# Five more quads of exponentials on VectorE, another filler for TensorE, and new ScalarE costs in the planner of a transformer block

## The chip, the cores and the metric

One core of a Trainium2 chip runs the kernel, in one launch. The metric is the time of one execution in microseconds on the device; less is better.

## What is computed

A transformer block with conditioning: layer norm and modulation, attention with 32 heads of 16, then layer norm, modulation and a gated feed-forward network (FFN), each with a gated residual. Cut to what matters (S = 2048, D = 512, H = 32, F = 1792, all bfloat16):

```python
mod = silu(c) @ w_mod                       # six rows of 512: sa, ca, ga, sb, cb, gb
h = layernorm(x) * (1 + ca) + sa
q, k, v = split(h @ wqkv)                   # 32 heads of 16
p = softmax(q @ k.T * 16 ** -0.5)           # 32 heads x 2048 x 2048
x = x + ga * ((p @ v) @ wo)
h = layernorm(x) * (1 + cb) + sb
x = x + gb * ((gelu(h @ w_gate) * (h @ w_up)) @ w_down)
```

The softmax has 32 x 2048 x 2048 exponentials, 134 million, or 2048 banks of 128 partitions by 512 columns.

## The kernel before, in words

The program is written by a planner that runs at build time. Every operation goes through `rec`, which finds its dependences and places it in a model of the engines' times (`model`, `cost`); `probe` asks when an operation could begin. `stream` is the planner's loop: at each turn it puts the next piece of TensorE work in order, and the order it finds is fixed in the program. No time is decided on the chip; engines wait for each other by semaphores.

Queries are cut into sets (`SETS`): seven of 256 queries and two of 128, where sets 0 and 1, and the last two, go together as 512 and 256 queries for the first four units. A unit is a set and one of eight groups of four heads (`qd`). A round of a unit is one bank of 512 columns for each of its four heads (`j`): scores are matmuls of kT against qT (even groups) or qo (odd groups) into `ps_sc`, six banks used as two sets of three (`CH`). ScalarE's exponential (`ACT.Exp`, through `act`, line 338) takes a set of two or three banks into a ring of 15 slots, `E`. Up to `nsplit` (the first two units, over all keys) every second set has two banks, because one bank holds the second unit's sum.

A round can instead be a quad: VectorE makes the bits of the bfloat16 exponential from each of its four banks (`ts` with `SHIFT_C`, line 350) into a `kq` buffer, one bank with each turn of the loop, so that ScalarE gets two banks and VectorE the third. The approximation is averaged over four shifts: three more buffers (`sq`) are made from `kq` by adding a number to the bits (`shift_task`, 128x2048), and each goes with a scaled copy of the values, `vs`. So a quad has 4 exps and 3 shifts on VectorE, and four times the PV matmuls of a plain round. Before, rounds were candidates for a quad (`cand`) only over the last four tiles of keys (`T0 = 12`), not in the first two units, and not until `modB` is there; `vs` holds those four tiles alone and is scaled when the last v is there (end of `side_v`).

PV matmuls (17 rows: 16 of v and a row of ones) add into `ps_pv`, or into the sixth score bank for the second unit (`pv_mms`, `acc_of`). When a unit ends, `unit_end` copies its sum to `osb` (line 359), and its sums of exponentials are inverted, spread through DRAM and multiplied in.

Side work is a list of generators with due positions (`plan`, `advance`): normalisation and q, k, v projections in the first stretch (`side_first`, `side_dc`, `side_q_all`), then for each set the output projection (`side_wo`), LN2 statistics and normalisation on VectorE (`ln2_steps`), its transposes (`side_t2`) and the FFN (`side_ffn`). It uses one bank, `ps_mi`, for its sums; `self.open` says that a sum is open there. The rate is a credit that grows with the position. VectorE's small work waits in `tasks`, taken by urgency (`step`).

`short` counts the columns that TensorE streamed in a window before now. Where they are under `FILL`, the planner adds filler: matmuls of the identity with one tile of xs, into a free score bank, or into `ps_mi` if no sum is open there.

Of the kernel before, what the change touches and what calls it, by code (L numbers as in the profile page):

```python
# [35 lines left out]
QJ = 4  # L36
QS = 4
MERGED = (((0, 1), (2, 3), (4, 5), (6,), (7,)), ((0, 1), (2, 3), (4,), (5,), (6,), (7,)))
CH = 3
# [5 lines left out]
NK = 4  # L45
CREDIT = 3500
NS = 3
# [8 lines left out]
MARGIN = {"db": 1200, "dd": 1800, "de": 1500, "qo": 1500, "st": 1500, "sd": 1700, "wd": 1700, "wu": 1500, "wg": 1500}  # L56
BACK = 6
GAP = 120
END = (0, None)
# [30 lines left out]
class _Recorder:  # L90
# [207 lines left out]
    def cost(self, eng, out, ins, kind):  # L298
        n = 1
        for _, k in (out if kind != "bn" else ins[0]).ap[1:]:  # L300
            n *= int(k)
        aps = [out] + list(ins)
        ps = any(self.kind.get(a.tensor.name) == "ps" for a in aps)
        small = all(mybir.dt.size(a.dtype) == 2 for a in aps)
        if eng == "act":
            return n * 0.833 + (51 if ps else 92)
        if eng == "pool":
            return n * 3.0 + 100
        f = 1
# [121 lines left out]
class _Kernel(_Recorder):  # L431
# [12 lines left out]
    def alloc(self):  # L444
# [35 lines left out]
        self.kq = [dreg[:, 0:2048], dreg[:, 2048:4096], mreg[:, 12288:14336]]  # L480
        self.kq += [sb("kq%d" % i, [P, 2048], BF16)[:, :] for i in range(3, NK)]
        self.vs = sb("vs", [P, len(SHIFT), NKT - T0, H * VW], BF16)
        self.wo = sb("wo", [P, 7, D], BF16)
        self.E = sb("E", [P, NSL, 512], BF16)
        self.onorm = sb("onorm", [P, 8, 512], BF16)
        self.ga = sb("ga", [P, D], BF16)
# [19 lines left out]
        self.rm = sb("rm", [P, 2], FP32)  # L506
        self.ident = sb("ident", [P, P], BF16)
        self.ones = dreg[:, 10 * D:10 * D + P]
        self.half = dreg[:, 10 * D + P:10 * D + 2 * P]
# [7 lines left out]
    def prologue(self):  # L517
# [19 lines left out]
        half = self.half  # L537
        self.memset(dve, self.warm, 0.0)
        self.memset(dve, half[:, 0:2], 0.5)
        self.memset(dve, self.ones, 1.0)  # L540
# [69 lines left out]
    def prologue_v(self):  # L610
        self.ln_stat(5)
        self.proj_v(0, 0, self.mi[:, :])
        for t in range(4, 6):
            self.done(("st", t))
# [150 lines left out]
    def side_v(self, g, dc):  # L765
# [61 lines left out]
    def side_first(self):  # L827
# [260 lines left out]
    def side_ffn(self, gi, part=None):  # L1088
# [66 lines left out]
        def U(ci):  # L1155
# [4 lines left out]
            for b0 in range(0, m, kpb):  # L1160
# [7 lines left out]
                yield END  # L1168
        early = [part is not None]

        def near():
            if early[0] and ("osb", gi + 1, 5) in self.have:
                early[0] = False
                yield from self.near_end(gi + 1, 5, self.mi)
# [102 lines left out]
    def plan(self, ends, nsplit, begin):  # L1277
# [78 lines left out]
    def stream(self):  # L1356
# [40 lines left out]
        last = {u: g0 + 4 for u, r, g0 in rounds}  # L1397
        begin = [min(g0 for u, r, g0 in rounds if u[1] // 2 == x) for x in range(4)]
        self.work = self.plan(ends, nsplit, begin)
        self.slot = {}  # L1400
# [8 lines left out]
        for u, r, g0 in rounds:  # L1409
# [4 lines left out]
        wait = []  # L1414
        self.quad_free = list(range(NK))
        self.sq_free = list(range(NSQ))
        cand = [k for k, (u, r, g0) in enumerate(rounds)
                if u not in units[:2] and r * (512 // u[3]) >= T0]
        quad = None

        def take(n):
# [57 lines left out]
        def pv_do(x):  # L1479
# [10 lines left out]
            else:  # L1490
# [4 lines left out]
                if q["n"] == 0:  # L1495
                    wait.remove(q)
                    self.quad_free.append(q["k"])
            if left[u] == 0:
# [6 lines left out]
        while cg <= group[units[-1]]:  # L1505
            if parts and pos >= max(loaded, ends[FLOW - 1] + 8):
                x = next((x for x in parts if all(k in self.have for k in x[2])), None)
                if x is not None:
# [3 lines left out]
                    loaded = pos + (8 if x[1][1] != 1 else 2)  # L1512
            t = max(self.pe_now(), virt)
            for k in range(NSETS):
                if pos >= ends[k]:
                    self.done(("qk", k))
# [9 lines left out]
            if tq is not None and tq <= t + 30:  # L1526
                slack = self.free["act"] - 600 - t
                w = self.next_side()
# [6 lines left out]
                g = None  # L1535
                if len(mem) == CH and "modB" in self.have and self.free["dve"] < max(t + 700, self.free["act"] + 150):
                    while quad is None and cand and last[rounds[cand[0]][0]] < pos + AHEAD[rounds[cand[0]][0][3] == 512]:
                        cand.pop(0)
                    overdue = {x[1][1] for x in self.tasks if x[1] is not None and x[1][0] == "shift" and self.plain[x[1][1]] <= LATE}
                    if quad is not None:  # L1540
                        if not overdue - {quad["rnd"][0]}:
                            g = quad["rnd"][2]
                    elif (not overdue and cand and self.quad_free and (pos < ends[FLOW - 1] or self.credit < CREDIT or (self.next_side() is None and self.waiting[0] in ("onorm", "osb"))) and rounds[cand[0]][2] < pos + 96 and self.backlog() < BACK
                          and ("vs", rounds[cand[0]][0][1] // 2) in self.have
                          and all(k in self.have for k in self.keys(seq[rounds[cand[0]][2]]))):
                        rnd = rounds[cand.pop(0)]
                        quad = {"rnd": rnd, "j": [0, 1, 2, 3], "k": self.quad_free.pop(0), "ready": [], "n": NS + 1, "slots": {}}
                        left[rnd[0]] += NS
# [25 lines left out]
                if g is not None:  # L1574
# [5 lines left out]
                    at = self.probe(bits)  # L1580
                    while self.free["dve"] + GAP < at and self.step("dve", self.free["dve"] + 40):
                        pass
# [22 lines left out]
            if w is not None and pos >= w[1]:  # L1605
                ts = self.probe(w[4][1])
                n = w[4][0]
                side = (ts <= t + 30 and (self.credit >= n / 2 or "last" in self.have or (self.short(t) > 0 and self.credit > -2048))
                        and n / 2.4 <= gap + max(0, self.free["act"] - 600 - t - max(0, gap)))
            if ok[0] and (ok[1] or self.pe_mode == 2 or tq is None or not mem) and not (  # L1610
# [37 lines left out]
    def pv_mms(self, rnd, acc, src, i, first, last):  # L1648
# [11 lines left out]
    def shift_task(self, q, i):  # L1660

        def f():
            s = self.sq_free[0]
            self.ts("dve", self.sq[s].bitcast(U16), self.kq[q["k"]].bitcast(U16), float(SHIFT[i]), None, ALU.add)
            if self.probing is None:
                self.sq_free.pop(0)
                q["slots"][i + 1] = s
                q["ready"].append((i + 1, [self.sq[s][:, 512 * x:512 * x + 512] for x in range(4)]))
        self.task([f], ("shift", q["rnd"][0]), lambda: bool(self.sq_free))

# [11 lines left out]
    def unit_end(self, u, acc):  # L1682
# [3 lines left out]
        self.copy("dve", self.osb[:, lo:hi], acc[:, 0:W])  # L1686
        if sets[0] >= NSETS - 2 and len(sets) == 1 and qd >= (6 if sets[0] == NSETS - 2 else 5):
# [4 lines left out]
        if two and qd % 2 == 0:  # L1692
            return
        us = [u]
        if two:
            us, lo, b = [(sets, qd - 1, q0, W), u], lo - W, b - 1
# [267 lines left out]
```

## Time and profile before

| | |
|---|---|
| median of 3 runs | 828.34 us (827.96 to 829.52) |
| the profiled execution's own time | 828.3 us |
| its span, first to last instruction | 826.5 us |
| mean granted TensorE clock | 0.989 |
| instructions | 37027 |

The span is shorter than the time by 1.8 us, which lie around it. In the profile PE is TensorE, PEld its weight loads, DVE VectorE, ACT ScalarE, POOL GpSimd and SP the queue that issues the transfers. A group is written line, engine, operation, out<-in with the names of the tiles; after the count come busy microseconds, the mean nanoseconds of one, and the idle time before them with what ended it. Lines are those of small helpers (325 is every matmul, 338 every activation, 350 every tensor_scalar), so groups are told apart by their tiles.

### The profile page before, as it was taken

To read this page: it belongs to the slowest core of one execution; us is meant where nothing else is said; L and a number is where in the kernel's file an instruction comes from. 1 tells how busy PE (TensorE), PEld (TensorE's weight loads), DVE (VectorE), ACT (ScalarE), POOL (GpSimd) and SP (SyncE) were. 2 spreads that over 40 slices of the span, in tenths; PEclk is the share of its full clock that TensorE was granted. 3 is DMA by queue.
4 is the path that set the end of the run, shared out by engine and by line. 5 is a ranking of instruction groups with operands and counts; after the bars stand their busy time and mean duration, and the time that the engine had idled before them with its cause. 6 is when DMAs were issued, how large, how long until landed. Compare 5 with 4: busy or idle time off the path is not lost.

```text
span 826.5 us, 37027 instructions
## 1 busy us (share of the span) xinstructions
PE 753.5 (91%) x17040; PEld 366.2 (44%) x17040; DVE 722.6 (87%) x1452; ACT 792.4 (96%) x746; POOL 4.5 (1%) x12
## 2 busy tenths in 40 slices
PE   8889899998989898999899989989899889988898
PEld 4333334333544444334444444344534443346557
DVE  7854878999999999999999799999988999979854
ACT  6999999999999999999999899999999999999982
POOL 2000000000000000000000000000000000000000
PEclk9989999999999999999999799999999999999999
DMA  9100000012451054103420243005423532200000
GB/s 299 53 12 13 10 9 11 10 27 59 136 146 33 16 161 121 40 10 110 125 86 16 78 130 97 25 22 164 110 68 107 178 93 66 72 10 11 18 12 13
DMA packets 94498, 57.35 MB, mean 69 GB/s; under 512 B 17030, under 2 KB 91911, under 8 KB 94343
## 3 DMA queue, kind: packets, MB, share of 16 engines
q1 hardware_dynamic: 93812, 54.47, 23.1%
q8 instruction: 133, 2.18, 1.1%
q10 hardware_dynamic: 530, 0.53, 0.2%
q14 instruction: 23, 0.18, 0.1%
HBM read 50.04 MB, written 2.35 MB: 63 GB/s over the span
## 4 chain that ended last, share of the span: by engine, by line
ACT 84%; PE 15%; DVE 1%; issue 1%
ACT E L338 81%; PE ps_sc L325 6%; PE ps_mi L325 5%; PE ps_pv L325 3%; ACT wreg L338 3%; PE ps_mi L329 0%; DVE mreg L350 0%; DVE xs L342 0%; DVE wreg L342 0%; DVE wreg L355 0%; PE ps_sc L329 0%; DVE wreg L350 0%; ACT hreg L338 0%; DVE osb L359 0%; DVE kT L359 0%
## 5 line engine op out<-in xcount | busy, mean ns | idle before, releaser
L338 ACT ACTIVATE E<-ps_sc 128x1024 bf16<-128x1024 f32 (+2 forms) x700 | 767.7, 1349 | 19.7 <-PE ps_sc L325 19.4
L325 PE MATMUL ps_sc<-qT,kT 32*128 32x256 bf16 (+3 forms) x2048 | 202.3, 275 | 26.7 <-ACT E L338 22.6
L325 PE MATMUL ps_sc<-qo,kT 32*128 32x256 bf16 (+2 forms) x2048 | 197.5, 274 | 27.1 <-ACT E L338 24.8
L325 PE MATMUL ps_pv<-E,vaug 128*17 128x256 bf16 (+2 forms) x3232 | 156.8, 275 | 1.0 <-DVE osb L359 0.7
L350 DVE TENSOR_SCALAR dreg<-ps_sc 128x512 uint16<-128x512 f32 x192 | 130.4, 685 | 13.9 <-PE ps_sc L325 13.2
L325 PE MATMUL ps_mi<-wreg,mreg 128*32 128x256 bf16 x2816 | 117.0, 277 | 4.2 <-DVE wreg L355 2.1
L325 PEld LDWEIGHTS ps_sc<-qT,kT 32*128 32x128 bf16 (+1 forms) x2048 | 62.1, 92 | 117.1 <-ACT E L338 101.9
L325 PEld LDWEIGHTS ps_sc<-qo,kT 32*128 32x128 bf16 x2048 | 59.9, 92 | 119.7 <-ACT E L338 111.6
L325 PEld LDWEIGHTS ps_pv<-E,vaug 128*17 128x17 bf16 x3232 | 60.5, 89 | 61.6 <-issue 40.8
L325 PEld LDWEIGHTS ps_mi<-wreg,mreg 128*32 128x32 bf16 x2816 | 64.7, 96 | 40.8 <-issue 25.5
L325 PE MATMUL ps_pv<-mreg,vs 128*17 128x256 bf16 (+2 forms) x1796 | 79.9, 269 | 2.1 <-issue 1.7
L350 DVE TENSOR_SCALAR mreg<-dreg 128x2048 uint16<-128x2048 uint16 x120 | 80.8, 682 | 1.0 <-PE ps_pv L325 0.8
L350 DVE TENSOR_SCALAR kq<-ps_sc 128x512 uint16<-128x512 f32 x96 | 65.2, 685 | 5.2 <-PE ps_sc L325 4.7
L350 DVE TENSOR_SCALAR mreg<-ps_sc 128x512 uint16<-128x512 f32 x96 | 65.2, 685 | 5.0 <-PE ps_sc L325 4.5
L325 PEld LDWEIGHTS ps_pv<-mreg,vs 128*17 128x17 bf16 x1796 | 40.0, 91 | 16.5 <-issue 6.5
L359 DVE CAST wreg<-ps_mi 128x512 bf16<-128x512 f32 x49 | 33.5, 684 | 5.2 <-PE ps_mi L325 4.2
L325 PE MATMUL ps_mi<-hreg,wreg 128*32 128x512 bf16 (+1 forms) x496 | 37.3, 384 | 0.5 <-DVE vaug L359 0.2
L355 DVE SCALAR_TENSOR_TENSOR wreg<-wreg,ps_mi 128x512 bf16<-128x512 bf16 x49 | 33.2, 678 | 1.9 <-ACT wreg L338 1.1
L342 DVE TENSOR_TENSOR wreg<-wreg 128x1024 bf16<-128x1024 bf16 (+1 forms) x56 | 34.3, 614 | 0.0
L350 DVE TENSOR_SCALAR mreg<-kq 128x2048 uint16<-128x2048 uint16 x48 | 32.1, 680 | 2.0 <-PE ps_pv L325 1.9
L350 DVE TENSOR_SCALAR mreg<-mreg 128x2048 uint16<-128x2048 uint16 x48 | 32.5, 677 | 0.1
L338 ACT ACTIVATE wreg<-wreg 128x1024 bf16<-128x1024 bf16 (+1 forms) x28 | 31.1, 1111 | 0.0
(171 smaller groups left out, 701.0 us busy)
## 6 DMA issues: line engine op xcount, KB each, us to landing
mreg<-in_B_w_up_dram SPq DMA_DIRECT2D x46, 256.0 KB, 3.0
mreg<-in_B_w_gate_dram SPq DMA_DIRECT2D x42, 256.0 KB, 3.1
dreg<-in_B_w_down_dram SPq DMA_DIRECT2D x18, 256.0 KB, 3.4
rb<-scr_rec SPq DMA_DIRECT2D x120, 32.0 KB, 2.3
mreg<-in_B_w_down_dram SPq DMA_DIRECT2D x12, 256.0 KB, 3.7
ereg<-in_B_w_down_dram SPq DMA_DIRECT2D x12, 256.0 KB, 3.5
mreg<-in_w_mod_dram SPq DMA_DIRECT2D x1, 2048.0 KB, 12.9
out_dram<-xs SPq DMA_DIRECT2D x15, 128.0 KB, 1.7
```

The source lines that it names most:

```text
L325: return self.rec("pe", lambda e: e.matmul(out, lhsT, rhs, start=start, stop=stop, tile_position=tp), [lhsT, rhs], [out], cost=(n, int(rhs ...
L338: return self.rec("act", lambda e: e.activation(out, in_, func, scale=scale, **kw), rd, wr, cost=self.cost("act", out, [in_], "act"))
L342: return self.rec(eng, lambda e: e.tensor_tensor(out, a, b, op), [a, b], [out], cost=self.cost(eng, out, [a, b], "tt"))
L350: return self.rec(eng, lambda e: e.tensor_scalar(out, a, s1, s2, **kw), rd, [out], cost=self.cost(eng, out, [a], "ts") + 60 * (len(rd) - 1 ...
L355: return self.rec("dve", lambda e: e.scalar_tensor_tensor(out, a, s, b, op0=op0, op1=op1), rd, [out], cost=self.cost("dve", out, [a, b], " ...
L359: return self.rec(eng, lambda e: e.tensor_copy(out, in_), [in_], [out], cost=self.cost(eng, out, [in_], "ts"))
```

## The change

- `cost`: ScalarE's cost in the planner is n x 0.8333 + 64 ns from PSUM and + 82 from SBUF (before, n x 0.833 + 51 and + 92).
- Quads may begin in the first two units: over the tiles from `4 * FIRST[dc]` on, for the first four units and all units of set 0. `vs` becomes four slots that hold the scaled copies of whichever key group was asked for last (`part_of`, `scale_v`, `holds`, `users`; `keyed` asks whether the copies are those of the round). For the early quads there are a fifth `kq` and two more `sq` buffers in onorm and ereg, which are not yet in use then (`room`).
- A filler of zeros: where TensorE is short, and the current unit's sum is open, four matmuls of a zero tile with a tile of xs add to it (`nought`).
- `STOP`: no quad begins while the side work waits for LN2 (`self.waiting[0]` is "ln2").
- The FFNs' due position is 20 earlier (+40 after the end of the last whole set instead of +60), and in the first stretch the statistics of tiles 8 to 11 may start after the normalisation of tiles 6 and 7 instead of after the first k.
- `TUNE`, `LONE` and `NEAR` hold constants that were written elsewhere; TUNE's 16 entries are the old values (600, CREDIT 3500, BACK 6, GAP 120), and LONE is 5 as before. NEAR drops a candidate of the first units that is under 6 positions away.

The diff, cut to its core:

```diff
-CREDIT = 3500
-BACK = 6
-GAP = 120
+LONE = max(5, QS)
+FIRST = (2, 2, 2, 3)
+STOP = ('ln2',)
+STOPAT = 0
+NEAR = 6
+TUNE = ((600, 3500, 6, 120),) * 16
...
-            return n * 0.833 + (51 if ps else 92)
+            return n * 0.8333 + (64 if ps else 82)
...
+        self.kq.append(onorm[:, 0:2048])
+        self.sq += [ereg[:, :], onorm[:, 2048:4096]]
...
+        self.memset(pool, self.zero[:, :], 0.0)
...
-        if 4 * g + 4 == NKT and not self.dry:
-            c = slice(VW * 8 * dc, VW * 8 * dc + VW * 8)
-            self.task([lambda i=i, o=o: self.ts("dve", self.vs[:, i, :, c], self.vaug[:, T0:NKT, c], float(2.0 ** (-o / 128)),
-                                                None, ALU.mult) for i, o in enumerate(SHIFT)], ("vs", dc))
+        self.scale_v(g, dc)
         yield END
+    def part_of(self, g, dc):
+        return dc + NKT // 4 - 1 - g
+    def scale_v(self, g, dc):
+        if self.dry or g < FIRST[dc]:
+            return
+        x = self.part_of(g, dc)
+        c, d = (slice(VW * 8 * x, VW * 8 * x + VW * 8) for x in (dc, x))
+        def scale(i, o):
+            if self.probing is None:
+                self.holds[x] = None
+            self.ts("dve", self.vs[:, i, :, d], self.vaug[:, 4 * g:4 * g + 4, c], float(2.0 ** (-o / 128)), None, ALU.mult)
+            if self.probing is None and i == NS - 1:
+                self.holds[x] = g, dc
+        self.task([lambda i=i, o=o: scale(i, o) for i, o in enumerate(SHIFT)], ("vs", dc, g), lambda: not self.users[x])
...
-            stats([8, 9, 10, 11], self.after([("k", 1, 0)]))
+            stats([8, 9, 10, 11], self.after([("ln", 1, 2)]))
...
-            e = ends[m] + 60
+            e = ends[m] - (-40)
...
         cand = [k for k, (u, r, g0) in enumerate(rounds)
-                if u not in units[:2] and r * (512 // u[3]) >= T0]
+                if r * (512 // u[3]) >= (4 * FIRST[u[1] // 2] if u in soon else T0)]
+        def room(pool, u):
+            if u in units[:2]:
+                ok = (3, 4) if pool is self.quad_free else (3, 4, 5)
+            elif "modB" not in self.have:
+                ok = (3,) if pool is self.quad_free else (3, 4)
+            else:
+                ok = range(NK if pool is self.quad_free else NSQ + (u in units[:4]))
+            return [x for x in pool if x in ok]
+        def keyed(k):
+            u, r, g0 = rounds[k]
+            g, dc = r * (512 // u[3]) // 4, u[1] // 2
+            return self.holds.get(self.part_of(g, dc)) == (g, dc)
...
-                if len(mem) == CH and "modB" in self.have and self.free["dve"] < max(t + 700, self.free["act"] + 150):
+                if len(mem) == CH and c > 2 and self.free["dve"] < max(t + 700, self.free["act"] + 150):
...
-                    elif (not overdue and cand and self.quad_free and (...) and rounds[cand[0]][2] < pos + 96 and self.backlog() < BACK
-                          and ("vs", rounds[cand[0]][0][1] // 2) in self.have
+                    elif (not overdue and cand and not (pos >= ends[STOPAT] and self.waiting[0] in STOP and self.next_side() is None) and room(self.quad_free, rounds[cand[0]][0]) and (...) and rounds[cand[0]][2] < pos + 96 and self.backlog() < self.tune[2]
+                          and keyed(cand[0])
...
+            if self.short(t) > 0 and pos < nseq:
+                u = next((u for u in units if group[u] == cg and u in begun and left[u] > 0), None)
+                if u is not None and gap > u[3] / 2.4:
+                    def nought():
+                        for j in range(4):
+                            self.mm(acc_of(u)[32 * j:32 * j + VW, 0:u[3]], self.zero[:, 0:VW], filler[1][:, 0:u[3]], start=False, stop=False, tp=(0, 32 * j))
+                    if self.probe(nought) <= t + 30:
+                        nought()
+                        continue
...
-            v = self.vs[:, i - 1, kt - T0, :] if i else self.vaug[:, kt, :]
+            v = self.vs[:, i - 1, kt % 4, VW * 8 * (self.part_of(kt // 4, dc) - dc):] if i else self.vaug[:, kt, :]
```

More of the change, by code (lines that the diff above doesn't have):

```diff
@@ L481, in alloc @@
         self.kq += [sb("kq%d" % i, [P, 2048], BF16)[:, :] for i in range(3, NK)]
+        onorm = sb("onorm", [P, 8 * 512], BF16)
+        self.onorm = onorm[:, :].rearrange("p (a n) -> p a n", a=8)
+        self.kq.append(onorm[:, 0:2048])
+        self.sq += [ereg[:, :], onorm[:, 2048:4096]]
         self.vs = sb("vs", [P, len(SHIFT), NKT - T0, H * VW], BF16)
@@ L484, in alloc @@
         self.E = sb("E", [P, NSL, 512], BF16)
-        self.onorm = sb("onorm", [P, 8, 512], BF16)
         self.ga = sb("ga", [P, D], BF16)
@@ L507, in alloc @@
         self.ident = sb("ident", [P, P], BF16)
+        self.zero = sb("zero", [P, P], BF16)
         self.ones = dreg[:, 10 * D:10 * D + P]
@@ L612, in prologue_v @@
         self.proj_v(0, 0, self.mi[:, :])
+        self.scale_v(0, 0)
         for t in range(4, 6):
@@ L1168, in U @@
                 yield END
-        early = [part is not None]
+        early = [part is not None and LONE == 5]
         def near():
-            if early[0] and ("osb", gi + 1, 5) in self.have:
+            if early[0] and ("osb", gi + 1, LONE) in self.have:
                 early[0] = False
@@ L1398, in stream @@
         begin = [min(g0 for u, r, g0 in rounds if u[1] // 2 == x) for x in range(4)]
+        self.tune = TUNE[0]
         self.work = self.plan(ends, nsplit, begin)
@@ L1414, in stream @@
         wait = []
-        self.quad_free = list(range(NK))
-        self.sq_free = list(range(NSQ))
+        self.quad_free = list(range(NK + 1))
+        self.sq_free = list(range(NSQ + 2))
+        self.holds = {}
+        self.users = [0] * (NKT // 4)
+        soon = units[:4] + [u for u in units[4:] if u[0] == (0,)]
         cand = [k for k, (u, r, g0) in enumerate(rounds)
-                if u not in units[:2] and r * (512 // u[3]) >= T0]
+                if r * (512 // u[3]) >= (4 * FIRST[u[1] // 2] if u in soon else T0)]
         quad = None
+        def room(pool, u):
[6 more added lines that the diff above has]
+            return [x for x in pool if x in ok]
+        self.room = room
+        def keyed(k):
+            u, r, g0 = rounds[k]
+            g, dc = r * (512 // u[3]) // 4, u[1] // 2
+            return self.holds.get(self.part_of(g, dc)) == (g, dc)
         def take(n):
@@ L1497, in pv_do @@
                     self.quad_free.append(q["k"])
+                    self.users[q["part"]] -= 1
             if left[u] == 0:
@@ L1513, in stream @@
             t = max(self.pe_now(), virt)
+            self.tune = TUNE[min(pos // P, 15)]
             for k in range(NSETS):
@@ L1526, in stream @@
             if tq is not None and tq <= t + 30:
-                slack = self.free["act"] - 600 - t
+                slack = self.free["act"] - self.tune[0] - t
                 w = self.next_side()
@@ L1535, in stream @@
                 g = None
-                if len(mem) == CH and "modB" in self.have and self.free["dve"] < max(t + 700, self.free["act"] + 150):
-                    while quad is None and cand and last[rounds[cand[0]][0]] < pos + AHEAD[rounds[cand[0]][0][3] == 512]:
-                        cand.pop(0)
+                while quad is None and cand and (rounds[cand[0]][2] < pos + NEAR if rounds[cand[0]][0] in soon else
+                                                 last[rounds[cand[0]][0]] < pos + AHEAD[rounds[cand[0]][0][3] == 512]):
+                    cand.pop(0)
+                if len(mem) == CH and c > 2 and self.free["dve"] < max(t + 700, self.free["act"] + 150):
                     overdue = {x[1][1] for x in self.tasks if x[1] is not None and x[1][0] == "shift" and self.plain[x[1][1]] <= LATE}
@@ L1542, in stream @@
                             g = quad["rnd"][2]
-                    elif (not overdue and cand and self.quad_free and (pos < ends[FLOW - 1] or self.credit < CREDIT or (self.next_side() is None and self.waiting[0] in ("onorm", "osb"))) and rounds[cand[0]][2] < pos + 96 and self.backlog() < BACK
-                          and ("vs", rounds[cand[0]][0][1] // 2) in self.have
+                    elif (not overdue and cand and not (pos >= ends[STOPAT] and self.waiting[0] in STOP and self.next_side() is None) and room(self.quad_free, rounds[cand[0]][0]) and (pos < ends[FLOW - 1] or self.credit < self.tune[1] or (self.next_side() is None and self.waiting[0] in ("onorm", "osb"))) and rounds[cand[0]][2] < pos + 96 and self.backlog() < self.tune[2]
+                          and keyed(cand[0])
                           and all(k in self.have for k in self.keys(seq[rounds[cand[0]][2]]))):
                         rnd = rounds[cand.pop(0)]
-                        quad = {"rnd": rnd, "j": [0, 1, 2, 3], "k": self.quad_free.pop(0), "ready": [], "n": NS + 1, "slots": {}}
+                        k = room(self.quad_free, rnd[0])[0]
+                        self.quad_free.remove(k)
+                        quad = {"rnd": rnd, "j": [0, 1, 2, 3], "k": k, "ready": [], "n": NS + 1, "slots": {},
+                                "part": self.part_of(rnd[1] * (512 // rnd[0][3]) // 4, rnd[0][1] // 2)}
+                        self.users[quad["part"]] += 1
                         left[rnd[0]] += NS
@@ L1580, in stream @@
                     at = self.probe(bits)
-                    while self.free["dve"] + GAP < at and self.step("dve", self.free["dve"] + 40):
+                    while self.free["dve"] + self.tune[3] < at and self.step("dve", self.free["dve"] + 40):
                         pass
@@ L1608, in stream @@
                 side = (ts <= t + 30 and (self.credit >= n / 2 or "last" in self.have or (self.short(t) > 0 and self.credit > -2048))
-                        and n / 2.4 <= gap + max(0, self.free["act"] - 600 - t - max(0, gap)))
+                        and n / 2.4 <= gap + max(0, self.free["act"] - self.tune[0] - t - max(0, gap)))
             if ok[0] and (ok[1] or self.pe_mode == 2 or tq is None or not mem) and not (
@@ L1662, in f @@
         def f():
-            s = self.sq_free[0]
+            s = self.room(self.sq_free, q["rnd"][0])[0]
             self.ts("dve", self.sq[s].bitcast(U16), self.kq[q["k"]].bitcast(U16), float(SHIFT[i]), None, ALU.add)
             if self.probing is None:
-                self.sq_free.pop(0)
+                self.sq_free.remove(s)
                 q["slots"][i + 1] = s
                 q["ready"].append((i + 1, [self.sq[s][:, 512 * x:512 * x + 512] for x in range(4)]))
-        self.task([f], ("shift", q["rnd"][0]), lambda: bool(self.sq_free))
+        self.task([f], ("shift", q["rnd"][0]), lambda: bool(self.room(self.sq_free, q["rnd"][0])))
     def osb_span(self, u):
@@ L1686, in unit_end @@
         self.copy("dve", self.osb[:, lo:hi], acc[:, 0:W])
-        if sets[0] >= NSETS - 2 and len(sets) == 1 and qd >= (6 if sets[0] == NSETS - 2 else 5):
+        if sets[0] >= NSETS - 2 and len(sets) == 1 and qd >= (6 if sets[0] == NSETS - 2 else LONE):
             self.done(("osb", sets[0], qd))
@@ L1691, in unit_end @@
         two = W == 256 and sets[0] < NSETS - 2 or len(sets) > 1 and sets[0]
-        if two and qd % 2 == 0:
+        if two and qd % 2 == 0 and (sets, qd + 1, q0, W) in self.units:
             return
         us = [u]
-        if two:
+        if two and qd % 2:
             us, lo, b = [(sets, qd - 1, q0, W), u], lo - W, b - 1
```

## The prediction

> **What bounds the kernel now.** I read the page from the top: busy time by engine, the slices, the chain that ended last, then ScalarE's groups with shapes kept apart, its waits, and a table by stretches.
>
> ```profile
> PE 753.5 (91%) x17040; PEld 366.2 (44%) x17040; DVE 722.6 (87%) x1452; ACT 792.4 (96%) x746; POOL 4.5 (1%) x12
> ACT  6999999999999999999999899999999999999982
> PEclk9989999999999999999999799999999999999999
> ACT 84%; PE 15%; DVE 1%; issue 1%
> L338 ACT ACTIVATE E<-ps_sc 128x1024 bf16<-128x1024 f32 x412 | 421.3, 1192 | 5.5 <-PE ps_sc L325 5.4
> L338 ACT ACTIVATE E<-ps_sc 128x1536 bf16<-128x1536 f32 x280 | 417.3, 1602 | 2.6 <-PE ps_sc L325 2.3
> ```
>
> ScalarE works for 96% of the span, it carries 84% of the chain, and nearly all of that is the exponential from score banks (ps_sc) to E. Its two big shapes take two or three banks of 512 columns at a time. The fourth bank of a set goes to VectorE where a "quad" (four banks of one round whose exponential VectorE makes from the bits) is under way.
>
> ```profile
> core 0: us, PE busy (x) PEld busy (x) DVE busy (x) ACT busy (x) POOL busy (x), PEclk, DMA share, GB/s
> 13.40:160.00 146.60, 130.57 (x2635) 53.35 (x2633) 107.42 (x245) 144.50 (x129) 0.31 (x1) 0.98 0.11 35
> 160.00:740.00 580.00, 535.06 (x12162) 252.89 (x12156) 546.21 (x1037) 575.96 (x542) 0.00 (x0) 0.99 0.29 82
> 740.00:800.00 60.00, 53.21 (x1844) 34.58 (x1836) 47.13 (x99) 58.59 (x52) 0.00 (x0) 1.00 0.06 12
> 800.00:826.50 26.50, 23.30 (x337) 19.57 (x325) 13.01 (x38) 7.24 (x14) 0.00 (x0) 0.98 0.05 15
> ACT E L338 <- PE ps_sc L325: 6.5, 14, 0.8
> ```
>
> The rows are the four stretches from the first exponential on, and then ScalarE's only kind of wait between 20 and 800 us: 6.5 us in 14 waits, all for scores. So from 13.4 to 800 us the time is ScalarE's work plus a few microseconds; what is taken off ScalarE there comes off the time, as long as nobody else fills the gap. VectorE has 39.2 us free in the first stretch (146.60 - 107.42), 33.8 in the second, 12.9 in the third. The last 26.5 us are a tail without big exponentials.
>
> **The terms, part by part.** First the price of a bank on ScalarE. Durations overlap (1192 ns is longer than the distance to the next start), so I take the chain, where each piece runs to the next start:
>
> ```profile
> 218.83 0.93 ACT wreg L338
> 219.76 4.03 ACT E L338 x3
> 744.13 0.93 ACT wreg L338
> 745.06 3.67 ACT E L338 x4
> ```
>
> The order of instructions says that the three after 219.76 all have 1536 columns and the four after 745.06 all have 1024. So 4.03/3 = 1.343 us and 3.67/4 = 0.918 us: a bank moved to VectorE saves 0.426 us of ScalarE.
>
> How many are moved I count in the order of the two built programs (counts, no times):
>
> ```
>                               before  after
> ACT E<-ps_sc 128x1536            280    260
> ACT E<-ps_sc 128x1024            412    432
> DVE 128x512 exps from ps_sc      384    404
> DVE 128x2048 shifts              288    303
> DVE vs<-vaug                      12     21
> PE 17-row matmuls (PV)          6496   6604
> PE zero fillers                    0     28
> ```
>
> Twenty banks, that is five quads, leave ScalarE: 20 x 0.426 = **8.5 us**. They don't lie where the name of the change suggests. At VectorE's copies of finished sums to osb (6 of 64 lie before 160 us, 49 up to 740 us) the count of VectorE exps is ahead by 10 after the sixth copy, by 15 after the 55th, and by 20 at the end. (Quads under way make this uncertain by 4.) So about 4.3 us of the gain belong to the first 160 us, 2.1 to the middle and 2.1 to the last units.
>
> What VectorE pays for it:
>
> ```profile
> L350 DVE TENSOR_SCALAR dreg<-ps_sc 128x512 uint16<-128x512 f32 x192 | 130.4, 685 | 13.9 <-PE ps_sc L325 13.2
> 564.02 0.68 DVE L350 TENSOR_SCALAR sq<-mreg 128x2048 uint16<-128x2048 uint16 x1
> 564.61 0.68 DVE L350 TENSOR_SCALAR mreg<-mreg 128x2048 uint16<-128x2048 uint16 x1
> 565.22 0.68 DVE L359 CAST wreg<-ps_mi 128x512 bf16<-128x512 f32 x1
> L350 DVE TENSOR_SCALAR vs<-vaug 128x544 bf16<-128x544 bf16 x12 | 2.8, 289 | 0.0
> ```
>
> Durations of 0.68 follow each other at 0.59 to 0.61 us, so an exp or a shift costs 0.60 and a vs scaling at most 0.29. Early: 10 exps, 9 shifts (the same count at the sixth copy) and 9 vs scalings, 14.0 us into 39.2 free. Middle: 5 exps and no more shifts, 3.0 us into 33.8. End: 5 exps and 6 shifts, 6.6 into 12.9. Each stretch has room, so I cost this at nothing; if it had none, rival 2 and 3 below give the price.
>
> ```profile
> L325 PE MATMUL ps_pv<-E,vaug 128*17 128x256 bf16 x2640 | 129.2, 275 | 1.0 <-DVE osb L359 0.7 <-DVE vaug L359 0.3
> ```
>
> TensorE gets 108 PV matmuls and 28 zeros more; four run side by side on 32 columns each. Even at the 275 ns that one 256-column matmul lasts, 136/4 x 0.275 = 9.4 us spread over 786, where TensorE stands free for 16.0 in the first stretch and 44.9 in the second (580.00 - 535.06). Nothing on the path; lower bound also nothing.
>
> ```profile
> 44.00:48.00 4.00, 2.70 (x30) 1.04 (x28) 2.48 (x7) 4.00 (x4) 0.00 (x0) 0.92 0.01 2
> 48.00:55.00 7.00, 7.00 (x102) 2.75 (x104) 1.69 (x3) 5.62 (x6) 0.00 (x0) 0.56 0.01 2
> 452.00:457.00 5.00, 3.82 (x84) 1.52 (x72) 3.41 (x13) 5.00 (x5) 0.00 (x0) 0.99 0.00 0
> 457.00:468.00 11.00, 10.95 (x154) 4.12 (x150) 6.27 (x13) 8.58 (x8) 0.00 (x0) 0.54 0.22 64
> PE ps_sc L325 <- ACT E L338: 1.5, 3, 0.7
> ```
>
> **Zeros into open sums, and LN2.** In these rows (TensorE, weight loads, VectorE, ScalarE busy; then the granted clock) the clock falls twice to about 0.55, after 4 to 5 us in which TensorE was busy for 68% and 76%. In the slow stretches TensorE is full and ScalarE stands for 1.38 us (7.00 - 5.62) and 2.42 us (11.00 - 8.58): 3.8 of its 6.5 us of waits. The old filler goes into ps_mi and is held back while a sum is open there; the new one adds zero weights to the open PV sum instead. The build places seven sets of four, three of them among the first hundred groups of TensorE's order, around the place of the first dip, none visibly at the second. At the second, TensorE is doing the LN2 transposes, with VectorE between; the rule that begins no quad while LN2 is due leaves VectorE to LN2 there. From nothing gone to 3.8 gone, I take one dip of the two, the mean of the pair: **1.9 us**. A new dip elsewhere would cost as much, so this term may be -3.8 to +3.8.
>
> The rest. ScalarE's costs in the planner (917 instead of 904 for two banks) come to what the chain shows, 0.918, and only change the order; they are the reason for more quads in the counts. Earlier statistics in the first loop, the FFN's due time 20 positions sooner, and the vs and buffer bookkeeping add no instruction beyond the table; the 466 transfer issues of SP are the same in number, and the tail has the same groups of up, gate and down matmuls. The other constants keep their values. Cost: nothing, bounds in the rivals.
>
> Sum against the profiled execution (826.5 us span, 828.3 us with what lies around it, and 828.34 the median of the three runs): 828.3 - 8.5 - 1.9 = **817.9 us**.
>
> **The rivals.**
> 1. *The dips stay.* They depend on something that fillers don't reach, and only the banks count: 828.3 - 8.5 = 819.8. The longest wait of TensorE between 40 and 56 us is 0.7 us (last row above), so no long pause explains the first dip, but 68% busy does; that speaks for the fillers. The Trainium skill, "TensorE: Matmul & The Clock Gate", section "HAM oscillation — how this bites in real kernels", gives as the abstract rule that gaps over about 3.4 us must be avoided. By that rule no dip could come from 0.7 us, and zeros would buy nothing; the trace does not agree with it. Chance 0.15.
> 2. *The first queries give nothing.* The 14.0 us of VectorE work early delay the casts of K and V, and scores come as late as ScalarE has become early; the 4.3 us there are lost: 828.3 - 8.5 + 4.3 = 824.1, with the dips as they were. For it: VectorE waits there for projections, as the rows below show, so part of the 39.2 is not free at the right moment. Chance 0.16.
>
> ```profile
> DVE vaug L359 <- PE ps_mi L325: 13.9, 10, 2.1
> DVE kT L359 <- PE ps_mi L325: 9.7, 8, 2.2
> ```
>
> 3. *Slower: VectorE sets the first 160 us.* Of 39.2 us free, 13.9 + 9.7 = 23.6 are waits for K and V projections, with which the next normalisation can only start afterwards. If only the other 15.6 can be filled and the added work falls in front of the casts, all 14.0 us stand in the way of K, V and then of scores: 828.3 - 8.5 + 14.0 = 833.8. It decides against the change from 8.5 us on that land on the path. Against it: ScalarE waited for only 2.6 us in that stretch (0.6 and 2.0 in the two shapes), and the planner puts quads where VectorE is free. Chance 0.10.
>
> ```profile
> L338 ACT ACTIVATE E<-ps_sc 128x1536 bf16<-128x1536 f32 x63 | 95.0, 1590 | 0.6 <-PE ps_sc L325 0.6
> L338 ACT ACTIVATE E<-ps_sc 128x1024 bf16<-128x1024 f32 x66 | 71.0, 1173 | 2.0 <-PE ps_sc L325 2.0
> ```
>
> 4. *All waits go*, 8.5 + 6.5: 813.3. Chance 0.08.
> 5. *It comes to nothing*: what ScalarE saves turns up as waits for scores, 828.3. Chance 0.05.
>
> **How the numbers follow.** The forecast has 0.46, the rivals 0.15, 0.16, 0.10, 0.08 and 0.05. The range of 8 in 10 runs from 812.0 (rival 4 less the 1.5 us by which the three runs differ) to 826.0 (rival 2 and half a dip more, 824.1 + 1.9); outside are rivals 3 and 5, 0.15 together. About 0.2%, 1.7 us, is what a measurement tells from no change: faster 0.85 (forecast, 1, 2, 4), same 0.05 (5), slower 0.10 (3).
>
> **What the profile after would show.** Right: the two shapes x260 and x432, ScalarE near 784 us busy (792.4 - 8.5), VectorE near 746 by durations of 0.68 (35 more of them), its waits for scores at 6 us or less, no clock below 0.9 near 50 us, and a first 160 us stretch that holds more of the order than before. Rivals 2 and 3 would show in ScalarE's waits between 20 and 160 us (4 or 14 us instead of 2), with K or V casts ahead of them in the chain. Rival 1 would show the dips in the same places with ScalarE's waits unchanged. The prediction is wrong if ScalarE's busy time falls by 8 us and its waits grow by more than that, or if the tail after the last big exponential is longer than 26.5 us: I count it as unchanged only by its instructions.

## The result and the profile after

The changed kernel takes 820.34 us (median of 4 runs, 818.21 to 820.93) against 828.15 us (median of 4, 827.51 to 829.52): a ratio of 0.9903, with a 95% interval of 0.988 to 0.9926. The forecast was 817.9 in a range of 812.0 to 826.0. The profiled execution took 820.56 us with a span of 817.5.

The page of the changed kernel, the same rows as before, then ScalarE's two shapes and its waits between 20 and 790 us (lines have moved by three: 341 is the activation, 328 the matmul, 353 tensor_scalar):

```profile
PE 750.5 (92%) x17184; PEld 366.4 (45%) x17188; DVE 742.8 (91%) x1496; ACT 783.2 (96%) x746; POOL 4.6 (1%) x13
PEclk9999999999999999999999999999999999999999
ACT 88%; PE 9%; DVE 1%; issue 0%; DMA 0%; SPq 0%; DVEq 0%
L341 ACT ACTIVATE E<-ps_sc 128x1024 bf16<-128x1024 f32 x432 | 434.9, 1169 | 2.0 <-PE ps_sc L328 2.0
L341 ACT ACTIVATE E<-ps_sc 128x1536 bf16<-128x1536 f32 x260 | 385.9, 1591 | 3.8 <-PE ps_sc L328 3.8
ACT E L341 <- PE ps_sc L328: 4.5, 8, 1.0
```

ScalarE's busy time fell by 9.2 us (792.4 to 783.2), VectorE's rose by 20.2 (722.6 to 742.8), and there is no slice with a lower clock. By stretch:

```profile
13.40:160.00 146.60, 133.73 (x2732) 54.10 (x2732) 120.65 (x273) 144.37 (x133) 0.31 (x1) 1.00 0.11 35
160.00:740.00 580.00, 536.00 (x12408) 257.06 (x12400) 557.70 (x1061) 580.00 (x548) 0.00 (x0) 1.00 0.29 82
740.00:791.50 51.50, 46.80 (x1690) 30.44 (x1678) 42.83 (x93) 47.38 (x44) 0.00 (x0) 1.00 0.07 15
791.50:817.50 26.00, 22.50 (x288) 19.12 (x291) 12.69 (x37) 5.64 (x11) 0.00 (x0) 1.00 0.05 14
```

In the middle ScalarE (the fourth busy column) has no gap at all; its remaining waits are one of 0.96 us at 125 us and 3.6 us between 740 and 790. VectorE's free time there went from 33.8 to 22.3 us.

The time falls into three parts: up to the first exponential, from it to the end of the last big one, and the tail. These are the ends, first of the kernel before and then of the changed one:

```profile
13.45 1.45 ACT L338 ACTIVATE E<-ps_sc 128x1536 bf16<-128x1536 f32 x1 [0.58 <-PE ps_sc L325]
777.26 22.84 ACT L338 ACTIVATE E<-ps_sc 128x1024 bf16<-128x1024 f32 x19 [0.39 <-PE ps_sc L325]
```

```profile
14.33 1.45 ACT L341 ACTIVATE E<-ps_sc 128x1536 bf16<-128x1536 f32 x1 [0.58 <-PE ps_sc L328]
784.03 5.48 ACT L341 ACTIVATE E<-ps_sc 128x1536 bf16<-128x1536 f32 x4 [0.81 <-PE ps_sc L328]
```

| | start | main | tail | outside the span | time |
|---|---|---|---|---|---|
| before | 13.4 | 786.7 | 26.4 | 1.8 | 828.3 |
| after | 14.3 | 775.2 | 28.0 | 3.1 | 820.6 |

The main part gained 11.5 us; 3.8 us were given back around it.

### The profile page after: what moved, and what is told of

The parts are those of the page before. It is cut to its first block, busy times and chain, and to the rows that moved or that the text cites. A ratio compares the mean times of both kernels' runs of the same rounds, so it can differ in the third digit from the quotient of the medians.

```text
span 817.5 us, 37365 instructions
## 1 busy us (share of the span) xinstructions
PE 750.5 (92%) x17184; PEld 366.4 (45%) x17188; DVE 742.8 (91%) x1496; ACT 783.2 (96%) x746; POOL 4.6 (1%) x13
## 3 DMA queue, kind: packets, MB, share of 16 engines
q1 hardware_dynamic: 93812, 54.47, 23.6%
## 4 chain that ended last, share of the span: by engine, by line
ACT 88%; PE 9%; DVE 1%; issue 0%; DMA 0%; SPq 0%; DVEq 0%
ACT E L341 85%; PE ps_sc L328 4%; PE ps_mi L328 3%; ACT wreg L341 3%; PE ps_pv L328 2%; DMA xs<-in_A_x_dram 0%; DVE osb L362 0%; DVE xs L345 0%; DVE dreg L353 0%; DVE st L381 0%; DVE wreg L353 0%; DVE nwt L345 0%; PE ps_sc L332 0%; DVE wreg L358 0%; DVE mreg L353 0%
## 5 line engine op out<-in xcount | busy, mean ns | idle before, releaser
L341 ACT ACTIVATE E<-ps_sc 128x1024 bf16<-128x1024 f32 (+2 forms) x700 | 758.7, 1319 | 19.1 <-PE ps_sc L328 19.0
L328 PE MATMUL ps_sc<-qo,kT 32*128 32x256 bf16 (+2 forms) x2048 | 202.2, 273 | 16.9 <-ACT E L341 15.5
L328 PE MATMUL ps_pv<-E,vaug 128*17 128x256 bf16 (+2 forms) x3204 | 154.1, 273 | 3.8 <-DVE osb L362 2.7
L353 DVE TENSOR_SCALAR dreg<-ps_sc 128x512 uint16<-128x512 f32 x200 | 135.5, 687 | 6.8 <-PE ps_sc L328 5.8
L328 PEld LDWEIGHTS ps_sc<-qo,kT 32*128 32x128 bf16 x2048 | 62.1, 92 | 105.6 <-ACT E L341 94.9
L353 DVE TENSOR_SCALAR kq<-ps_sc 128x512 uint16<-128x512 f32 x104 | 70.9, 688 | 8.6 <-PE ps_sc L328 8.2
L353 DVE TENSOR_SCALAR mreg<-dreg 128x2048 uint16<-128x2048 uint16 x100 | 67.5, 682 | 2.2 <-PE ps_pv L328 2.2
L353 DVE TENSOR_SCALAR mreg<-mreg 128x2048 uint16<-128x2048 uint16 x71 | 47.4, 686 | 0.0
L353 DVE TENSOR_SCALAR sq<-dreg 128x2048 uint16<-128x2048 uint16 x49 | 33.7, 687 | 0.8 <-PE ps_pv L328 0.8
```

Source lines behind the costliest of these rows:

```text
L328: return self.rec("pe", lambda e: e.matmul(out, lhsT, rhs, start=start, stop=stop, tile_position=tp), [lhsT, rhs], [out], cost=(n, int(rhs ...
L341: return self.rec("act", lambda e: e.activation(out, in_, func, scale=scale, **kw), rd, wr, cost=self.cost("act", out, [in_], "act"))
L353: return self.rec(eng, lambda e: e.tensor_scalar(out, a, s1, s2, **kw), rd, [out], cost=self.cost(eng, out, [a], "ts") + 60 * (len(rd) - 1 ...
```

## The experiments

All runs have runs of the kernel before on the same chip beside them, so ratios are compared; the changed kernel itself was not run again. In the first six kernels (five headings) the order of instructions is that of the parent, word for word; in the others the planner plans anew. A dip is a stretch of a trace in which TensorE's granted clock is at half. The edits are shown shortened.

**Zeros narrowed, order kept.**

```diff
-self.mm(acc[.., 0:u[3]], self.zero[:, 0:VW], filler[1][:, 0:u[3]], start=False, stop=False, ..)
+matmul(acc[.., 0:1], self.zero[:, 0:VW], filler[1][:, 0:1], start=False, stop=False, ..)   # planned at the old cost
```

> The changed kernel with its order kept word for word, but each of the 28 zero matmuls streams 1 column instead of 256 or 512 (the planner is told the old length, so nothing else moves). The prediction's theory (zeros keep TensorE busy enough for the clock): the dip near 50 us comes back, about 7 us at half clock, ScalarE waits 1.4 us more there, 821.5 to 824. Rival (the new order alone removed the dips, zeros do nothing): 820.3 as with the change, within 0.8, clock at 1.0 throughout.

820.77 us, ratio 0.9915 (0.9885 to 0.9944). The stretches around 50 us, of the narrowed kernel:

```profile
44.00:48.00 4.00, 3.03 (x34) 1.23 (x34) 3.06 (x11) 4.00 (x5) 0.00 (x0) 1.00 0.01 2
48.00:55.00 7.00, 6.59 (x124) 2.65 (x121) 4.27 (x7) 7.00 (x9) 0.00 (x0) 1.00 0.01 2
```

Clock 1.00 and ScalarE full in both: no dip here without the zeros. The trace has one dip, of 3.4 us at 16 us; it stands at the same place in the trace of the changed kernel with repeated shifts (below), which has its zeros whole, so it isn't owed to them. The rival held but for the clock, which is 0.990 to 1.000 over the eight runs and not 1.0 throughout. What the zeros are worth is too small to be measured here: the two ratios, 0.9915 and 0.9903, each have an interval of about 0.003 either way.

**All fillers narrowed, order kept.** The same edit on the old fillers too, 43 sets in all.

> The changed kernel, order kept, with all 43 fillers (36 sets of identity times xs, 7 sets of zeros) streaming 1 column instead of 256 or 512. The run with only the zeros narrowed kept its time and its clock. If the old fillers are what holds the clock, dips of 3.4 to 10 us come back at several places, each 1 to 3.5 us: 823 to 830. If the new order alone holds it, 820 to 821 with no dip between 30 and 780 us.

829.5 us, ratio 1.0044 (1.0027 to 1.0061), mean clock 0.975 in the profiled run: more than the whole gain is gone. Six dips lie in this trace between 20 and 780 us, of 3.4 to 10.2 us, and each begins within 1.5 us of a narrowed set of the old filler. The first dip of the kernel before is one of them. These are its stretches, then the set of old filler ahead of it, as it is in the changed kernel and as it is here:

```profile
44.00:48.00 4.00, 3.06 (x62) 1.41 (x60) 3.12 (x12) 4.00 (x5) 0.00 (x0) 1.00 0.00 0
48.00:55.00 7.00, 6.56 (x56) 2.03 (x53) 3.37 (x6) 5.66 (x6) 0.00 (x0) 0.58 0.01 4
```

```profile
47.19 0.40 PE L328 MATMUL ps_sc<-xs,ident 128*32 128x512 bf16 x4
```

```profile
48.13 0.19 PE L329 MATMUL ps_sc<-xs,ident 128*32 128x1 bf16 x4
```

The clock is at 0.58 and ScalarE stands for 1.34 us (7.00 - 5.66). The kernel before has no filler at this place. So at the first dip it is a set of the old filler, which the new order puts there, that holds the clock; whether the zeros beside it would have done it alone was not tried. The second dip, which was at 457 us, does not come back:

```profile
440.00:500.00 60.00, 54.67 (x1366) 28.44 (x1358) 58.09 (x116) 60.00 (x57) 0.00 (x0) 1.00 0.34 96
```

In the changed kernel no filler runs between 403 and 466 us either, so in these traces the second dip went by the new order and not by a filler. All fillers together are worth about 12.6 us (829.5 against 0.9903 x 824.9, the kernel before beside it).

**The kernel before without its dips, order kept.**

```diff
+AGAIN = ((441, 600), (8821, 8983))           # TensorE's instructions ahead of the two dips
+if eng == "pe" and reads[0].tensor.name == "kT" and in AGAIN: issue the matmul twice
```

> The kernel before, order kept, but score matmuls in the two stretches ahead of its dips (39 to 52 us and 448 to 457 us) are done twice, 66 matmuls more, which TensorE's idle time there can hold. Prediction's theory: both dips go and with them ScalarE's 3.8 us of waits, 824.4. Second theory, from the progress of the two traces (between the unit that ends at 457 us and the one at 488 us the change gains 6.6 us): a dip costs more than the waits it shows, 819 to 822. Rival (the clock goes by something else than how busy TensorE is): 828 as before, dips still there.

825.52 us, ratio 0.9974 (0.9954 to 0.9995).

```profile
48.00:55.00 7.00, 6.56 (x130) 2.82 (x130) 2.87 (x6) 7.00 (x7) 0.00 (x0) 1.00 0.01 2
457.00:468.00 11.00, 10.43 (x251) 5.19 (x248) 9.74 (x18) 11.00 (x12) 0.00 (x0) 1.00 0.37 104
```

Both dips are gone, and ScalarE is full where it stood for 1.38 and 2.42 us. The main part is 783.0 us instead of 786.7: the two dips cost 3.7 of it, what ScalarE's waits had said (3.8), and not the 6.6 that I read from the progress of two traces with different orders. The median gained less, 2.1 us by the ratio. Most runs of the kernel before had fewer dips than its profiled one (the 26 beside this have a median clock of 0.996, the profiled one 0.989), and some runs of this kernel still have dips (0.993 to 1.0).

**ScalarE's work in the changed kernel, order kept.** 11 two-bank exponentials are done twice, with nothing told to the planner:

```diff
 one(); self.nexp += 1
+if self.nexp % 40 == 20: self.again("act", one)     # the engine's planned time is restored after it
```

> The changed kernel, order kept, with 11 of the 432 two-bank exponentials done twice, spread evenly. If ScalarE sets the time all through, 11 x 0.92 = 10.1 us more, somewhat over that if the second one waits for the first: 830 to 832. Rival (the time is now set by VectorE or TensorE over long stretches, and ScalarE only looks full): less than half, under 825.

833.44 us, ratio 1.0072 (1.005 to 1.0094): 12.7 us over the narrowed zeros run beside it, 1.15 for each. In the trace a repeated exponential starts 1.09 to 1.25 us after the first, and what follows it 0.92 later, so the eleven take 12.9 us of ScalarE's time and all of it comes through: ScalarE sets the time. (Its runs have somewhat more dips, mean clock 0.988 to 0.998, so a part may be theirs.)

**VectorE's work in the changed kernel and in the kernel before, order kept.** Every eighth shift is done twice, 37 and 36:

```diff
 one(); self.nshift += 1
+if self.nshift % 8 == 0: self.again("dve", one)
```

> The changed kernel, order kept, with 37 of the 303 VectorE shifts done twice, spread evenly: 37 x 0.60 to 0.70 = 22 to 26 us more VectorE work, about what the change itself added. Prediction's theory (VectorE has room in every stretch, its work costs nothing): at most 2 us more, 820 to 822.5. Rival (VectorE is at its limit): 10 us or more, 830 and up.

> The kernel before, order kept, with 36 of its 288 shifts done twice, as in the run of the changed kernel with 37, which took some 15 us longer instead of the 2 I had expected. If the change used up a reserve that VectorE had before, this one costs much less: under 6 us, below 834. If work that the planner did not plan falls on VectorE's path in both kernels alike (free time there is not free at the moment that counts), it costs 12 to 16 us here too: 840 to 843.

The changed kernel: 835.26 us, ratio 1.0081 (1.0053 to 1.0109), 14.5 over the narrowed zeros run beside it. The kernel before: 834.67, ratio 1.0081 (1.005 to 1.0113), 6.5 over its own. In the traces a repeated shift starts 0.72 us after the first, so 27 and 26 us of work cost 14.5 and 6.5 us, 0.39 and 0.18 an instruction. The chain that ended last runs over VectorE for 48% and 27% of the span, against 1% in both kernels without the repeats. ScalarE's waits between 20 and 790 us, first the changed kernel with 37 and then the kernel before with 36:

```profile
ACT E L346 <- PE ps_sc L333: 11.8, 35, 1.0
```

```profile
ACT E L343 <- PE ps_sc L330: 9.2, 23, 0.8
```

These are 35 and 23 short waits instead of 8 and 14. My expectation for the changed kernel, 2 us, was wrong by far, and of the two theories for the kernel before neither held alone: VectorE's free time was never free for work put in blindly, and in the changed kernel such work costs about twice as much as before.

**Parts, planned anew.** The kernel before with the new ScalarE costs alone; the changed kernel with the old costs; and without early quads (`cand` as before, `FIRST` 3):

```diff
-            return n * 0.833 + (51 if ps else 92)
+            return n * 0.8333 + (64 if ps else 82)
```

> The kernel before with nothing but the new ScalarE costs in the planner; it plans anew and moves 8 banks (272 and 420 instead of 280 and 412). By banks alone 8 x 0.426 = 3.4 us: 824, with dips as chance has them 821 to 825. Rival (the order that the planner falls into matters more than the banks): anything from 822 to 831, no relation to the 3.4.

> The changed kernel with the old ScalarE costs; planned anew it has 268 and 424, so 12 banks moved instead of 20. By banks: 8 x 0.426 = 3.4 us slower than the changed kernel, 823 to 825. Rival as for the kernel before with the new costs: order decides, 819 to 828.

> The changed kernel without quads in the first queries (candidates as before, not in the first two units and not before modB, no key groups below 12); planned anew it still has 264 and 428, 16 banks moved of the 20. By banks: 4 x 0.426 = 1.7 us slower than the changed kernel, 822. If the early quads are what brings the gain, as the name of the change has it, 4.3 us slower or more, 824.5 and up.

And the changed kernel without `STOP`, and, as a control, with the FFN due one position later:

> The changed kernel without the rule that begins no quad while LN2 is due (STOP empty); planned anew, with the same 20 banks moved (260 and 432). If the rule keeps TensorE's side work from running dry, there are dips or waits for scores of 2 us or more in the stretches of LN2: 822.5 to 827. If the banks are all that counts: 820 to 821.

> A control: the changed kernel with the FFN due one position later (41 instead of 40), which means nothing by itself but makes the planner fall into another order, again with 260 and 432. The difference from the changed kernel's 820.3 is what a new order alone is worth: by the runs so far (main stretches of 783 to 786 us at 12 to 16 banks moved) up to 4 us either way, 819 to 824.5.

| kernel | banks moved | median | before, beside it | ratio (95%) | mean clock of its runs |
|---|---|---|---|---|---|
| before, new costs | 8 | 828.38 | 828.12 | 1.0008 (0.9985 to 1.0031) | 0.987 to 0.998 |
| after, old costs | 12 | 826.36 | 828.12 | 0.9979 (0.9961 to 0.9996) | 0.992 to 0.998 |
| after, no early quads | 16 | 826.70 | 828.12 | 0.9977 (0.9948 to 1.0006) | 0.986 to 1.000 |
| after, no STOP | 20 | 825.19 | 824.93 | 1.0000 (0.9984 to 1.0017) | 0.987 to 1.000 |
| after, due 41 | 20 | 825.98 | 824.93 | 1.0009 (0.9985 to 1.0034) | 0.986 to 1.000 |
| after | 20 | 820.34 | 828.15 | 0.9903 (0.988 to 0.9926) | 0.998 to 1.000 |

Every part taken out loses the gain or nearly all of it, none of the forecasts by banks came, and a part that means nothing does the same: with the due position at 41 the same 20 banks are moved, and the time is that of the kernel before. Compared by ratios (1.0009 against 0.9903) the control is about 8.7 us slower than the changed kernel; I had allowed 4. What differs is in the last column. The control's run at a clock of 1.000 took 820.42 us, its two slowest, at 0.986 and 0.989, took 831.08; the kernel without early quads took 821.03 and 822.12 at 1.000 and 831.65 at 0.986. One of the control's dips:

```profile
764.00:769.00 5.00, 4.04 (x160) 3.06 (x152) 3.29 (x9) 4.09 (x4) 0.00 (x0) 0.99 0.07 12
769.00:779.00 10.00, 9.96 (x194) 5.70 (x197) 6.26 (x15) 7.45 (x7) 0.00 (x0) 0.50 0.02 3
```

So single parts can't be priced by planning anew: each order has its own places where the clock can fall, and whether it does changes from run to run. Clock doesn't explain all: the kernel before with new costs has only one dip in its trace, of 3.4 us at 16 us, took 826.04 in that run, and its main part is 783.3, where 8 banks and both dips off 786.7 would give 779.6.

**A version meant to be faster.**

```diff
-TUNE = ((600, 3500, 6, 120),) * 16
+TUNE = ((600, 3000, 6, 120),) * 16
```

> A version meant to be faster: the changed kernel with quads allowed only at a credit under 3000 columns instead of 3500 in the last sets, 16 banks moved (264 and 428). By banks alone 1.7 us slower than the changed kernel, 822; if the order it falls into has fewer waits for scores, 816 to 820.

817.41 us, ratio 0.9902 (0.9883 to 0.9922). Its profiled run had a span of 813.9, no dip, 2.7 us of waits and a tail of 25.6 instead of 28.0; but by the ratio it can't be told from the change, with 16 banks moved instead of 20.

## Why the prediction was right, point by point

- *Twenty banks, 8.5 us.* The counts came as written (260 and 432), and ScalarE's busy time fell by 9.2; the other 0.7 goes with the dips (without them the kernel before has 791.7 instead of 792.4). That ScalarE's work passes to the time one to one, the run with repeated exponentials shows. From the kernel before without dips (main 783.0) to the changed one (775.2) are 7.8 us. They also lie about where the prediction put them (4.3 us early, 6.4 up to 740 us, 8.5 in all): counted from the first exponential, the seventh copy to osb comes 3.3 us sooner than in the kernel before without dips (144.4 against 147.7), the 55th 5.2 (712.2 against 717.4).
- *Dips, 1.9 us for one of two.* Both went, worth 3.7 in the profiled runs. The term was mis-sized by half, and its reason was wrong: rival 1's first half, that the zeros don't matter, is what the narrowed zeros show. At the first dip the old filler in a new order holds the clock, at the second the new order alone. Which part of the change did that at the second (the rule on LN2 was the prediction's other reason) stays open, and chance may have a hand in it: the trace of the kernel before with repeated shifts has only the first dip. Rival 1's other half, that the dips stay and no filler reaches them, fell. The Trainium skill, "TensorE: Matmul & The Clock Gate", section "HAM oscillation — how this bites in real kernels", has the abstract rule of no gaps over about 3.4 us. It doesn't cover this kernel: the dip at 47 us came with no wait of TensorE over 0.7 us.
- *VectorE's work at nothing.* In the sum this came out; as a claim that the free time is room it failed (0.39 us for each unplanned shift). The planned work fits, presumably because the planner puts it where nobody waits. Rivals 2 and 3 didn't come: up to 160 us ScalarE waits only 0.67 and 0.96 us after the first exponential, and VectorE's waits for K and V projections fell from 23.6 to 11.0 us (rows below), about as much as VectorE's busy time rose there (13.2 us), so the added work went mostly into them.

```profile
DVE kT L362 <- PE ps_mi L328: 5.8, 7, 1.5
DVE vaug L362 <- PE ps_mi L328: 5.2, 8, 1.6
```

- *The rest only changes the order, at nothing.* This is the step that failed in kind: the control shows that another order with the same banks costs about 8.7 us. Its median lies 5.6 us above its own run at a clock of 1.000, so by that one run dips make up the larger part. The two orders run alike up to the 24th of the 64 copies to osb (344.5 and 344.4 us after the first exponential in the two traces); it falls back after that. That the forecast was near is in part luck: the four runs of the changed kernel have clocks of 0.998 to 1.000, the control's twelve a median of 0.993, and no count could tell.
- *What was given back.* 828.3 - 8.5 - 3.7 is 816.1; the profiled run took 820.6. The start was 0.9 us later, which is chance: with the same order the narrowed zeros' first exponential is at 13.3. The time outside the span was 1.3 more (over the four runs it is 1.9 to 3.1). The tail is 1.6 longer: the prediction had counted it unchanged by its instructions, and had named a tail over 26.5 us as a sign that it is wrong. That sign came, at 28.0, and it belongs to the order: the four other traces of this order have 28.1 to 28.3, the two others of the order before 26.3 and 26.4. In the next rows, before and after, the last sum is copied 0.85 us after the last big exponential (800.96 after 800.11) and then 1.68 (791.19 after 789.51), since two shifts and the matmuls of the last quad still stand in front of it. That makes half of the 1.6; what makes the other half stays open. And 0.7 is left in the main part, where ScalarE's waits are 4.5 us against 3.7 in the kernel before without its dips.

```profile
800.96 0.29 DVE L359 COPY osb<-ps_pv 128x128 f32<-128x128 f32 x1
```

```profile
788.31 0.69 DVE L353 TENSOR_SCALAR mreg<-dreg 128x2048 uint16<-128x2048 uint16 x1 [2.07 <-PE ps_pv L328]
789.12 0.68 DVE L353 TENSOR_SCALAR sq<-dreg 128x2048 uint16<-128x2048 uint16 x1
791.19 0.29 DVE L362 COPY osb<-ps_pv 128x128 f32<-128x128 f32 x1 [0.78 <-PE ps_pv L328]
```

Open: what the rule on LN2, the due time and the early quads do by themselves. Their removal changes the order, and an order-keeping form of them was not tried.

## What to carry to other kernels

When a build-time planner fixes the order, price the work by counts, but test a single part with the order kept (repeat or narrow an instruction in place), and run a meaningless control before believing a part's difference. Free time of an engine beside the bound is not a reserve: here one more VectorE instruction cost a quarter of its length in one order and half of it in the other. Where TensorE is not the bound, its clock may still cost time, so read the clock of several runs of the same program, and look at what TensorE does in the 4 us ahead of each dip.

## What the runs showed of the hardware

The dips in these traces up to 780 us last 3.4, 6.8 or 10.2 us. The four whose rows are shown, here and in the prediction, follow stretches with TensorE busy for 68% to 81% of 4 or 5 us. But that share alone doesn't tell: this stretch of the changed kernel has 59%, and no dip came.

```profile
638.00:642.00 4.00, 2.36 (x64) 1.29 (x56) 4.00 (x10) 4.00 (x4) 0.00 (x0) 1.00 0.86 278
```

What else decides stays open. Over runs of the same kernel before, 0.001 of mean clock goes with 0.44 to 0.54 us (straight lines through three sets of 23 to 29 runs, from 0.984 to 0.998). At 826 us, 0.001 is 1.65 us at half the clock, so about 0.3 us is lost for each; the rest doesn't reach the time. I had not expected that the same program has its dips in some runs and not in others: the control's twelve runs range from 820.42 to 831.08 us with the clock.
